# Quarter products of the last batch: one two-bank PSUM tile for two chains of sums, or a tile for each chain

## The chip, the cores and the metric

The kernel runs on one core of one Trainium2 chip. The metric is the device time in microseconds of one execution; the kernel before has a median of 998.69 us over three runs (998.07 to 1000.25). TensorE (PE) does the matrix products, its weight loads are shown as PEld; ScalarE (ACT) and VectorE (DVE) take results out of PSUM and do the arithmetic between products; GpSimd (POOL) and the DMA queues play no part in the stretch that is changed.

## The reference

Routing attention over 4 batches, 8 heads, 768 tokens of 64 numbers, followed by a two-layer network with a leaky slope per hidden unit:

```python
mask = q_assign[:, :, :, None] == k_assign[:, :, None, :]   # nearest of 16 centroids
scores = np.where(mask, scale * q @ k.T, -1e9)
attn = softmax(scores)
x = (attn @ v) as (3072, 512)
h = x @ w_in                                    # w_in  512 x 2048
g = np.maximum(h, 0.0) + alpha * np.minimum(h, 0.0)
out = g @ w_out                                 # w_out 2048 x 512
```

All of it is fp32.

## The kernel before, in words

The attention of one batch is computed while the two-layer network of the batch before it is fed in between in small pieces. The order of the instructions on each engine is the order of the program text (the pools are under a manual schedule); an engine executes its instructions in that order, and a tile pool adds the waits that its buffers and data need. Every buffer of a pool is given out in turn, and the first write to it waits until the last reader of its previous tile is done.

When the attention of all four batches has ended, the network of the last batch alone is left, and TensorE has nothing else to do. It is written by `last_pieces` (line 1089) and cuts each of the two matrix products in 2 x 2 quarters, so that seven quarter products are enough where eight would be needed, at the price of sums and differences on VectorE before and after. It has two stages.

**Hidden stage, `hidden(x)`, x = 0 to 7 ("blocks" here).** A block makes two tiles of 128 hidden units (x and 8 + x) for the 768 tokens of the batch, in halves of 384 tokens. It issues seven products. Each is two matmul instructions in the program and four matmul records in the trace (fp32), 128 x 384 wide. Two of the results are partial sums that are read out and then added to, in place, in PSUM:

- chain "a": products p1, p6, p7 and p4 into one PSUM area. p1 is copied out by ScalarE, then p6 is added to it and the sum is copied out by ScalarE, then p7 is added and VectorE adds the sum to a tile, then p4 is added and the last sum is copied out by ScalarE. Each read must be over before the next product of the chain writes.
- chain "e": products p5 and p3. p5 is copied out by ScalarE; p3 is added to it and VectorE adds the sum to a tile.
- "z": product p2 alone, which VectorE adds to a tile.

The order on TensorE is p1, p5, p2, p4 of the block before (it is put off by one block, list `late`), p6, p3, p7. Chains "a" and "e" are the two halves (bank 0 and bank 1) of one tile `two` of the pool `ps_s`, which has two such tiles; "z" comes from `ps_f`, which has two tiles of one bank.

VectorE does, for each block, in this order: the addition after p2, the slope (line 1129) of the block before after its p4, the addition after p3, a slope, the addition after p7, and then for x > 1 the sums that the second product needs of block x - 2: `g_sums` (4 operations, line 1168) and `w_out_sums` (4 operations, line 1177), and in blocks 2 and 4 also `w_in_sums` (4 wider ones, line 1080).

**Between the stages, `room_for_y`** runs the last p4 and the sums of blocks 6 and 7.

**Final stage, `final(t)`, t = 0 to 2.** Each t makes two row tiles of the output, again by seven products; here a product is 8 matmul instructions (16 records), 128 x 256 wide, one for each block x, in that order. The order is p1, p2, p5, p6, p3, p7 for t = 0 (p4 is put off into the next t), and p1, p5, p6, p2, p7, p3, p4 for t = 1 and 2. Chain "a" is p1, p6, p7, p4; chain "e" is p5, p3; "z" is p2. The copies are by ScalarE (line 1121), the additions by VectorE (line 1124), as before. p5 of t = 0 is the first product that reads what `g_sums` and `w_out_sums` made: its matmuls for x = 6 and x = 7 need the sums of `room_for_y`.

The pool `ps_v` (one tile of one bank) holds the attention's weighted sums and is not used in this part of the program before the change.

Of the kernel before, what the change touches and what calls it, by code (L numbers as in the profile page):

```python
# [10 lines left out]
FP32 = mybir.dt.float32  # L11
# [8 lines left out]
P = 128  # L20
# [3 lines left out]
def kernel(  # L24
# [20 lines left out]
    HS = HJ * P  # L45
# [26 lines left out]
    ps_s = fast.enter_context(tc.tile_pool(name="ps_s", bufs=2, space=PS))  # L72
    ps_v = fast.enter_context(tc.tile_pool(name="ps_v", bufs=1, space=PS))
    ps_m = fast.enter_context(tc.tile_pool(name="ps_m", bufs=1, space=PS))
    ps_f = fast.enter_context(tc.tile_pool(name="ps_f", bufs=2, space=PS))
# [984 lines left out]
    KH, NQ, HC = NCH // 2, NF // 2, DM // 2  # L1060
# [32 lines left out]
    def last_pieces():  # L1093
# [4 lines left out]
        def places():  # L1098
# [18 lines left out]
            s4.extend(t[:, h * HS:(h + 1) * HS] for t in more for h in range(2))  # L1117
            assert len(s4) >= NQ

        def copy(to, of):  # L1120
            nc.scalar.copy(to, of)

        def plus(to, of):
            nc.vector.tensor_tensor(out=to, in0=to, in1=of, op=ALU.add)
# [7 lines left out]
        def w_in_form(m, x, cc):  # L1132
            f1, f2 = (slice(f * P, (f + 1) * P) for f in (x, NQ + x))
            if m in ("11", "12"):
                return w_in_sb[:, cc + KH * (m == "12"), f1]
            if m in ("22", "S3"):
                return w_in_sb[:, cc + KH * (m == "22"), f2]
            t = by_pair[x // 2].rearrange("p (m c w) -> p m c w", m=3, c=KH)
            return t[:, ("S1", "S2", "S4").index(m), cc, (x % 2) * P:(x % 2 + 1) * P]

        def g_sum(x, m):

            if m == "S4":
                return s4[x]
            t = by_pair[x // 2].rearrange("p (x m q) -> p x m q", x=2, m=2)
            return t[:, x % 2, ("S1", "S2").index(m)]
# [8 lines left out]
        def w_out_form(m, x):  # L1155
            if m in ("11", "21", "22"):
                c0 = HC * (m == "22")
                return w_out_sb[:, x if m == "11" else NQ + x, c0:c0 + HC]
            i = ("T1", "T2", "T3", "T4").index(m)
            f = x + NQ * (i // 2)  # L1160
            return w_in_sb[:, KH * (i % 2):KH * (i % 2 + 1), f * P:(f + 1) * P]

        def g_sums(x):
            (t0, t1), (z0, z1) = g[x][0], g[NQ + x][0]
            S1, S2, S4 = (g_sum(x, m) for m in ("S1", "S2", "S4"))
            for to, p, q, op in ((S1, t1, z1, ALU.add), (S2, S1, t0, ALU.subtract),
                                 (t1, t0, t1, ALU.subtract), (S4, z0, S2, ALU.subtract)):
                nc.vector.tensor_tensor(out=to, in0=p, in1=q, op=op)

        def w_out_sums(x):  # L1170

            T1, T2, T3, T4 = (w_out_form(m, x) for m in ("T1", "T2", "T3", "T4"))
            B11, B12, B21, B22 = (
                w_out_sb[:, f, c0:c0 + HC].rearrange("p (a w) -> p a w", a=KH)
                for f in (x, NQ + x) for c0 in (0, HC))
            for to, p, q in ((T1, B12, B11), (T2, B22, T1), (T3, B22, B12), (T4, B21, T2)):
                nc.vector.tensor_tensor(out=to, in0=p, in1=q, op=ALU.subtract)
# [3 lines left out]
        def hidden(x):  # L1181
            f1, f2 = x, NQ + x
            bank = {}

            def product(to, m, rhs, start):
                if to == "a" and start:
                    two = ps_s.tile([P, 2, 512], FP32, name="sps")
                    bank["a"], bank["e"] = two[:, 0, 0:HS], two[:, 1, 0:HS]
                if to == "z":
                    bank["z"] = ps_f.tile([P, 512], FP32, name="fps")[:, 0:HS]  # L1190
                for cc in range(KH):
                    nc.tensor.matmul(out=bank[to], lhsT=w_in_form(m, x, cc),  # L1192
                                     rhs=rhs[:, cc, :], start=start and cc == 0,
                                     stop=cc == KH - 1, skip_group_check=not start)
                return bank[to]

            def x_of(half, kh):
                return xTs[b, half][:, kh * KH:(kh + 1) * KH]

            def g_of(f, half):  # L1200
                return g[f][0][half]

            def p1():
                if not g:
                    places()
                copy(g_of(f1, 0), product("a", "11", x_of(0, 0), True))

            def p5():
                copy(g_of(f2, 1), product("e", "S1", x_sums[0], True))

            def p2():
                plus(g_of(f1, 0), product("z", "12", x_of(0, 1), True))
                if late:
                    late.popleft()()

            def p6():
                copy(g_of(f1, 1), product("a", "S2", x_sums[1], False))

            def p3():
                plus(g_of(f1, 1), product("e", "S4", x_of(1, 1), False))  # L1220
                slopes(f1)

            def p7():
                plus(g_of(f2, 1), product("a", "S3", x_of(1, 0), False))
                late.append(p4)
                if x % 2 == 0 and x:
                    g_sums(x - 2)
                    w_out_sums(x - 2)
                    if x // 2 + 1 < NQ // 2:
                        w_in_sums(x // 2 + 1)  # L1230
                elif x > 1:
                    g_sums(x - 2)
                    w_out_sums(x - 2)

            def p4():
                copy(g_of(f2, 0), product("a", "22", x_sums[2], False))
                slopes(f2)
            return [p1, p5, p2, p6, p3, p7]

        def final(t):  # L1240
            bank = {}
            y0, y1 = (lambda c0, i=i: ys[i][:, c0:c0 + HC] for i in (t, HJ + t))

            def product(to, m, n, start):
                if to == "a" and start:
                    two = ps_s.tile([P, 2, 512], FP32, name="sps")
                    bank["a"], bank["e"] = two[:, 0, 0:HC], two[:, 1, 0:HC]
                if to == "z":
                    bank["z"] = ps_f.tile([P, 512], FP32, name="fps")[:, 0:HC]
                for x in range(NQ):  # L1250
                    nc.tensor.matmul(out=bank[to], lhsT=g_form(m, x, t),  # L1251
                                     rhs=w_out_form(n, x), start=start and x == 0,
                                     stop=x == NQ - 1, skip_group_check=not start)
                return bank[to]

            def store(i, c0, c1):
                nc.sync.dma_start(out=rows[:, i, c0:c1], in_=ys[i][:, c0:c1])

            def p1():
                copy(y0(0), product("a", "11", "11", True))  # L1260
                while late:
                    late.popleft()()

            def p5():
                copy(y1(HC), product("e", "S1", "T1", True))

            def p6():
                copy(y0(HC), product("a", "S2", "T2", False))

            def p2():  # L1270
                plus(y0(0), product("z", "12", "21", True))

            def p7():
                plus(y1(HC), product("a", "S3", "T3", False))
                if t == HJ - 1:
                    store(HJ + t, HC, DM)

            def p3():
                plus(y0(HC), product("e", "S4", "22", False))
                store(t, 0, DM)  # L1280

            def p4():
                copy(y1(0), product("a", "22", "T4", False))
                store(HJ + t, 0, HC if t == HJ - 1 else DM)
            if t == 0:
                return [p1, p2, p5, p6, p3, p7, lambda: late.append(p4)]
            return [p1, p5, p6, p2, p7, p3, p4]

        def room_for_y():
            late.popleft()()  # L1290
            t = xpool.tile([P, NCH, HS], FP32, name="xT").rearrange("p c q -> p (c q)")
            ys.extend(ypool.tile([P, DM], FP32, name="y") for _ in range(HJ))
            ys.extend(t[:, i * DM:(i + 1) * DM] for i in range(HJ))
            for x in (NQ - 2, NQ - 1):
                g_sums(x)
                w_out_sums(x)
        pieces = []
        for x in range(NQ):
            pieces += hidden(x)
        pieces.append(room_for_y)  # L1300
        for t in range(HJ):
            pieces += final(t)
# [246 lines left out]
    for i in (1, 3):  # L1549
# [25 lines left out]
                     start=True, stop=True)  # L1575
# [162 lines left out]
```

## Time and profile before

| what | before |
|---|---|
| median of 3 runs | 998.69 us |
| the profiled execution | 993.32 us, its span 991.5 us |
| PE busy | 952.9 us, 96% of the span |
| DVE busy / ACT busy | 69% / 26% |
| granted TensorE clock | 1.00 |
| hidden stage of the last batch | from 810.21 us to 904.92 us |
| final stage | from 904.92 us to 985.5 us |

The span is counted from the first to the last instruction of the profiled execution; that execution took 1.8 us more than its span, and its time is 5.4 us below the median of the timed runs. A row of the timeline gives the start, the length, the engine, the line, what is written and read, how many instructions are merged, and in square brackets how long the engine had been idle before it and who ended that. The lengths of matmuls are modelled and overlap: a product's own cost is read from the distance of two starts.

### The profile page before, as it was taken

The numbers are of one execution on the slowest core, as the hardware profiler recorded it, in microseconds if no ns is written. First come the engines' busy times: TensorE is split into PE (matmuls) and PEld (weight loads), VectorE is DVE, ScalarE is ACT, GpSimd is POOL, SyncE is SP. The second block draws the span as 40 slices with busy tenths as digits, with TensorE's granted clock in tenths as the row PEclk, the third lists the DMA queues.
The fourth block names the chain that finished last, engine by engine and source line by source line (L and its number), as shares of the span: only waits on it lengthen the run. The fifth ranks groups of instructions, "written<-read, shape, count | busy, mean of one in ns | idle before, by whom it ended". The sixth has DMA issues, their size and how long they took to land.

```text
span 991.5 us, 11208 instructions
## 1 busy us (share of the span) xinstructions
PE 952.9 (96%) x4059; PEld 498.9 (50%) x4059; DVE 684.0 (69%) x1241; ACT 259.5 (26%) x474; POOL 215.0 (22%) x249
## 2 busy tenths in 40 slices
PE   8999999999999999999999999999999998888997
PEld 5534444454454544545445454544545544446775
DVE  5897789798486886878867786687997353777000
ACT  5674534222220222302222022221322101111000
POOL 1432222110002624310000383510255410000000
PEclk9999999999999999999999999999999999999999
DMA  7442666080201654126020221803511120000000
GB/s 283 149 115 90 136 154 106 2 157 40 53 1 51 168 87 84 39 61 85 1 33 1 82 67 38 154 11 52 85 34 33 32 55 0 0 1 1 21 22 25
DMA packets 175583, 64.67 MB, mean 65 GB/s; under 512 B 161360, under 2 KB 165152, under 8 KB 175520
## 3 DMA queue, kind: packets, MB, share of 16 engines
q1 hardware_dynamic: 170064, 55.62, 25.4%
q0 software_dynamic: 4608, 7.87, 2.4%
q8 instruction: 34, 0.56, 0.2%
q10 hardware_dynamic: 848, 0.39, 0.2%
q14 instruction: 29, 0.24, 0.1%
HBM read 45.15 MB, written 18.35 MB: 64 GB/s over the span
## 4 chain that ended last, share of the span: by engine, by line
PE 89%; DVE 5%; ACT 2%; issue 1%; DMA 1%; POOL 0%; SPq 0%; DVEq 0%; ACTq 0%
PE fps L1017 25%; PE fps L1035 25%; PE vps L893 9%; PE sps L757 8%; PE sps L1192 7%; PE sps L1251 7%; PE fps L757 3%; PE fps L1251 1%; PE fps L1192 1%; DMA vt<-in_v_dram 1%; PE vps L926 1%; PE mps L381 1%; PE sps L766 1%; PE mps L926 1%; DVE power L265 0%
## 5 line engine op out<-in xcount | busy, mean ns | idle before, releaser
L1017 PE MATMUL fps<-xT,w_in_sb 128*128 128x384 f32 x768 | 259.2, 491 | 0.0
L1035 PE MATMUL fps<-w_out_sb,gT 128*128 128x512 f32 x576 | 256.0, 597 | 1.1 <-DVE gT L1009 1.1
L1017 PEld LDWEIGHTS fps<-xT,w_in_sb 128*128 128x128 f32 x768 | 142.3, 190 | 103.9 <-ACT more L778 4.4
L663 POOL DMA_INDIRECT scratch<-stage,off x96 | 102.3, 1066 | 323.2 <-DMA stage<-in_v_dram 269.5
L1035 PEld LDWEIGHTS fps<-w_out_sb,gT 128*128 128x128 f32 x576 | 106.9, 190 | 127.2 <-issue 117.4
L1023 ACT COPY gT<-fps 128x384 f32<-128x384 f32 x96 | 45.9, 478 | 224.2 <-PE fps L1017 224.2
L757 PE MATMUL sps<-qkT 64*128 64x384 f32 (+1 forms) x512 | 96.1, 494 | 0.0
L798 DVE SCALAR_TENSOR_TENSOR more<-aq,key,more 128x384 f32<-128x384 bf16 (+1 forms) x136 | 74.4, 605 | 29.5 <-ACT more L778 19.2
L1009 DVE SCALAR_TENSOR_TENSOR gT<-gT,alpha 128x384 f32<-128x384 f32 x96 | 61.3, 647 | 35.7 <-ACT gT L1023 35.5
L778 ACT ACTIVATE E<-sps 128x768 f32<-128x768 f32 (+1 forms) x81 | 61.2, 802 | 71.1 <-PE sps L766 38.4
L963 POOL DMA_INDIRECT back<-rows,place x48 | 47.5, 990 | 101.0 <-ACT rows L958 87.6
L757 PEld LDWEIGHTS sps<-qkT 64*128 64x128 f32 x512 | 45.7, 186 | 44.5 <-issue 17.4
L798 DVE SCALAR_TENSOR_TENSOR E<-aq,key,E 128x384 f32<-128x384 bf16 (+1 forms) x104 | 56.6, 601 | 16.1 <-ACT E L778 11.4
L893 PE MATMUL vps<-E,vt 128*64 128x384 f32 x356 | 65.7, 494 | 1.5 <-DVE xT L993 1.5
L808 DVE TENSOR_TENSOR acc<-acc,E 128x768 f32<-128x768 f32 x47 | 44.9, 955 | 14.8 <-ACT E L778 13.6
L778 ACT ACTIVATE more<-sps 128x768 f32<-128x768 f32 (+1 forms) x47 | 35.4, 796 | 41.3 <-PE sps L757 40.8
L271 POOL TENSOR_TENSOR w_in_sb<-w_in_sb,power 128x512 f32<-128x512 f32 x16 | 25.7, 1611 | 69.6 <-DVE w_in_sb L268 69.6
L893 PEld LDWEIGHTS vps<-E,vt 128*64 128x64 f32 x356 | 23.0, 136 | 33.4 <-issue 31.0
L893 PE MATMUL vps<-more,vt 128*64 128x384 f32 x220 | 38.8, 491 | 0.0
L1041 ACT COPY y<-fps 128x512 f32<-128x512 f32 x18 | 10.5, 586 | 101.2 <-PE fps L1035 101.2
L271 POOL TENSOR_TENSOR w_out_sb<-w_out_sb,power 128x512 f32<-128x512 f32 x16 | 22.5, 1410 | 56.0 <-DVE w_out_sb L268 56.0
L757 PE MATMUL fps<-qkT 64*128 64x384 f32 x160 | 34.5, 508 | 0.0
(267 smaller groups left out, 1072.9 us busy)
## 6 DMA issues: line engine op xcount, KB each, us to landing
raw<-in_moe_w_in_dram SPq DMA_DIRECT2D x16, 512.0 KB, 4.8
raw<-in_moe_w_out_dram SPq DMA_DIRECT2D x16, 512.0 KB, 3.8
out_dram<-y SPq DMA_DIRECT2D x21, 256.0 KB, 2.2
vt<-in_v_dram SPq DMA_DIRECT2D x12, 384.0 KB, 4.2
qk<-in_q_dram SPq DMA_DIRECT2D x48, 96.0 KB, 3.7
qk<-in_k_dram SPq DMA_DIRECT2D x48, 96.0 KB, 3.7
w_in_kept<-w_in_sb SPq DMA_DIRECT2D x8, 512.0 KB, 3.8
qk<-scratch SPq DMA_DIRECT2D x32, 96.0 KB, 3.4
```

The costliest lines, as they stand in the source:

```text
L271: nc.gpsimd.tensor_tensor(out=dst, in0=dst, in1=power[0].bitcast(FP32), op=ALU.mult)
L663: nc.gpsimd.indirect_dma_start(out=scratch[n][1][h * NX + xx], out_offset=bass.IndirectOffsetOnAxis(ap=ranks[n][:, xx, h:h + 1], axis=0), ...
L757: nc.tensor.matmul(out=bank(ps, h, m), lhsT=qkT[r:r + D, S + c * P:S + (c + 1) * P], rhs=qkT[r:r + D, tokens], start=True, stop=not early_ ...
L778: nc.scalar.activation(out=E[:, :, 0:m], in_=ps[:, :, 0:m], func=AF.Exp, scale=SCALE)
L798: nc.vector.scalar_tensor_tensor(out=e, in0=of, scalar=keys[n][:, NJ + c, h:h + 1], in1=e, op0=ALU.is_equal, op1=ALU.mult)
L893: nc.tensor.matmul(out=po[r:r + D, 0:HS], lhsT=vts[n][:, h, c, :], rhs=e[:, h, :], start=(c == 0), stop=(c == NJ - 1))
L963: nc.gpsimd.indirect_dma_start(out=to[i], out_offset=bass.IndirectOffsetOnAxis(ap=place[:, h, j:j + 1], axis=0), in_=rows[:, j, h * D:(h + ...
L1009: nc.vector.scalar_tensor_tensor(out=gs[f], in0=gs[f], scalar=alpha[:, f:f + 1], in1=gs[f], op0=ALU.mult, op1=ALU.max)
L1017: nc.tensor.matmul(out=ps[:, 0:HS], lhsT=w_in_sb[:, c, f * P:(f + 1) * P], rhs=xTs[b, half][:, c, :], start=(c == 0), stop=(c == NCH - 1))
L1035: nc.tensor.matmul(out=ps[:, 0:DM], lhsT=gs[f][:, i * P:(i + 1) * P], rhs=w_out_sb[:, f, :], start=on and f == f0, stop=off and f == f0 + ...
L1192: nc.tensor.matmul(out=bank[to], lhsT=w_in_form(m, x, cc), rhs=rhs[:, cc, :], start=start and cc == 0, stop=cc == KH - 1, skip_group_check ...
L1251: nc.tensor.matmul(out=bank[to], lhsT=g_form(m, x, t), rhs=w_out_form(n, x), start=start and x == 0, stop=x == NQ - 1, skip_group_check=no ...
```

## The change

The two chains no longer share a tile. Chain "a" takes one tile of `ps_s` and uses its first bank only; chain "e" takes the one tile of `ps_v`; "z" takes a tile of `ps_f` as before. This holds for both stages. In `room_for_y` the four `g_sums` operations of blocks 6 and 7 come first, and then the `w_out_sums` of both, where the two kinds alternated by block.

```diff
+        def new_bank(to):
+            if to == "a":
+                return ps_s.tile([P, 2, 512], FP32, name="sps")[:, 0, :]
+            pool, name = (ps_v, "vps") if to == "e" else (ps_f, "fps")
+            return pool.tile([P, 512], FP32, name=name)
...
             def product(to, m, rhs, start):
-                if to == "a" and start:
-                    two = ps_s.tile([P, 2, 512], FP32, name="sps")
-                    bank["a"], bank["e"] = two[:, 0, 0:HS], two[:, 1, 0:HS]
-                if to == "z":
-                    bank["z"] = ps_f.tile([P, 512], FP32, name="fps")[:, 0:HS]
+                if start:
+                    bank[to] = new_bank(to)[:, 0:HS]
...
             def product(to, m, n, start):
-                if to == "a" and start:
-                    two = ps_s.tile([P, 2, 512], FP32, name="sps")
-                    bank["a"], bank["e"] = two[:, 0, 0:HC], two[:, 1, 0:HC]
-                if to == "z":
-                    bank["z"] = ps_f.tile([P, 512], FP32, name="fps")[:, 0:HC]
+                if start:
+                    bank[to] = new_bank(to)[:, 0:HC]
...
             for x in (NQ - 2, NQ - 1):
                 g_sums(x)
+            for x in (NQ - 2, NQ - 1):
                 w_out_sums(x)
```

No product moves on TensorE, but what its products wait for does. Here is TensorE in block 3 of the hidden stage before the change, with the waits that stand in the program (an engine's name stands for a semaphore that it counts up); the rows are p1, p5, p2, p4 of block 2, p6, p3 and p7, and a product's second instruction is left out:

```order
L1192 MATMUL sps_5256<-xT_4756,w_in_sb_61 128x384 x2
L1192 MATMUL sps_5256<-vt_5096,qkT_5084 128x384 [waits Activation_49]
...
L1192 MATMUL fps_5263<-xT_4756,w_in_sb_61 128x384 x2
L1192 MATMUL sps_5218<-vt_5098,w_in_sb_61 128x384 [waits DVE_49]
...
L1192 MATMUL sps_5256<-vt_5097,qkT_5084 128x384 [waits Activation_49]
...
L1192 MATMUL sps_5256<-xT_4758,qkT_5084 128x384 [waits Activation_49]
...
L1192 MATMUL sps_5256<-xT_4758,w_in_sb_61 128x384 [waits DVE_49]
```

And the same products after it:

```order
L1195 MATMUL sps_5259<-xT_4756,w_in_sb_61 128x384 x2
L1195 MATMUL vps_5263<-vt_5096,qkT_5084 128x384 [waits DVE_49]
...
L1195 MATMUL fps_5267<-xT_4756,w_in_sb_61 128x384 x2
L1195 MATMUL sps_5220<-vt_5098,w_in_sb_61 128x384 [waits DVE_49]
...
L1195 MATMUL sps_5259<-vt_5097,qkT_5084 128x384 [waits Activation_49]
...
L1195 MATMUL vps_5263<-xT_4758,qkT_5084 128x384 [waits Activation_49]
...
L1195 MATMUL sps_5259<-xT_4758,w_in_sb_61 128x384 [waits Activation_49]
```

p5 no longer waits for ScalarE (the copy of p1, which reads the other half of the shared tile) but for VectorE: the one tile of `ps_v` must have been read by the addition after p3 of block 2. p7 no longer waits for VectorE (the addition after p3, other half) but for ScalarE: the copy of p6 in its own chain. p3 waits for ScalarE in both, before for the copy of p6, now for the copy of p5.

The second place is VectorE in `room_for_y`, before:

```order
L1168 TENSOR_TENSOR vt<-gT,qkT 128x384
L1177 TENSOR_TENSOR w_in_sb<-w_out_sb 128x2x128
L1177 TENSOR_TENSOR w_in_sb<-w_out_sb,w_in_sb 128x2x128
L1177 TENSOR_TENSOR w_in_sb<-w_out_sb 128x2x128
L1177 TENSOR_TENSOR w_in_sb<-w_out_sb,w_in_sb 128x2x128
L1168 TENSOR_TENSOR qkT<-gT 128x384
L1168 TENSOR_TENSOR qkT<-qkT,gT 128x384
L1168 TENSOR_TENSOR gT<-gT 128x384
L1168 TENSOR_TENSOR vt<-gT,qkT 128x384
L1177 TENSOR_TENSOR w_in_sb<-w_out_sb 128x2x128
```

and after:

```order
L1174 TENSOR_TENSOR vt<-gT,qkT 128x384
L1174 TENSOR_TENSOR qkT<-gT 128x384
L1174 TENSOR_TENSOR qkT<-qkT,gT 128x384
L1174 TENSOR_TENSOR gT<-gT 128x384
L1174 TENSOR_TENSOR vt<-gT,qkT 128x384
L1183 TENSOR_TENSOR w_in_sb<-w_out_sb 128x2x128
```

The first row is the end of `g_sums` of block 6. The first `w_out_sums` operation of block 6 stands four operations later than before, the first `g_sums` operation of block 7 four earlier, and the first `w_out_sums` operation of block 7 (the last row of the upper list) in the same place as before, as the ninth after the first row.

## The prediction

> **What bounds the kernel now.** I read the windows first, to see which engine limits the stretch that is changed, then PE's waits there, then the timeline for the price of each wait, and last VectorE's timeline, because the change hands it a wait. The first window is the network of the batch before, the second the hidden stage, the third the final stage.
>
> ```profile
> core 0: us, PE busy (x) PEld busy (x) DVE busy (x) ACT busy (x) POOL busy (x), PEclk, DMA share, GB/s
> 760.00:800.00 40.00, 39.47 (x145) 21.05 (x144) 20.23 (x35) 5.56 (x12) 21.42 (x22) 1.00 0.12 29
> 810.00:905.00 95.00, 79.53 (x228) 40.57 (x227) 54.54 (x110) 14.83 (x31) 0.00 (x0) 1.00 0.02 6
> 905.00:985.00 80.00, 74.77 (x336) 62.65 (x335) 13.46 (x33) 4.57 (x12) 0.00 (x0) 1.00 0.05 19
> ```
>
> PE is busy 39.47 of 40 us just before, then 79.53 of 95 and 74.77 of 80. No other engine is near full: VectorE has 54.54 of 95. So PE has gaps without a busier engine behind them; some chain goes to and fro between engines. PE's waits from 810 us on name it:
>
> ```profile
> engine line waited for: us in total, times, longest us
> PE sps L1192 <- ACT more L1121: 3.4, 6, 0.6
> PE sps L1192 <- ACT E L1121: 2.3, 4, 0.6
> ...
> PE sps L1192 <- DVE more L1124: 2.2, 3, 0.7
> PE sps L1251 <- DVE y L1124: 1.8, 3, 0.6
> ```
>
> PE waits for the engines that read its own results out of the shared tile, twice for ScalarE's copy and once for VectorE's addition in each hidden block. These idle times are too small as prices, since a matmul's modelled length overlaps the wait. The price is the distance of two starts less the product's own cost. Block 3, from p5 to the p5 of block 4:
>
> ```profile
> 846.31 1.56 PE L1192 MATMUL sps<-vt,qkT 128*128 128x384 f32 x4 [0.57 <-ACT more L1121]
> 847.71 1.45 PE L1192 MATMUL fps<-xT,w_in_sb 128*128 128x384 f32 x4
> 849.00 1.45 PE L1192 MATMUL sps<-vt,w_in_sb 128*128 128x384 f32 x4
> 850.28 1.45 PE L1192 MATMUL sps<-vt,qkT 128*128 128x384 f32 x4
> 852.31 1.56 PE L1192 MATMUL sps<-xT,qkT 128*128 128x384 f32 x4 [0.57 <-ACT more L1121]
> 854.58 2.85 PE L1192 MATMUL sps<-xT,w_in_sb 128*128 128x384 f32 x8 [0.72 <-DVE more L1124]
> 858.00 1.56 PE L1192 MATMUL sps<-vt,qkT 128*128 128x384 f32 x4 [0.57 <-ACT more L1121]
> ```
>
> A product costs 1.29 us (847.71 to 849.00 to 850.28). The block takes 858.00 - 846.31 = 11.69 us, seven products 9.03, so 2.66 us are lost. Split: p5 to p3 is four products, 5.16, and takes 6.00, so p3 loses 0.84; p3 to p7 takes 2.27 for 1.29, so p7 loses 0.98; p7 with the next p1 takes 3.42 for 2.58, so p5 loses 0.84.
>
> **The change, part by part.**
>
> *Hidden stage, three waits per block.* Each wait that is left after the change must be over before its product's turn. ScalarE first; the second copy is that of p6:
>
> ```profile
> 850.49 0.48 ACT L1121 COPY E<-sps 128x384 f32<-128x384 f32 x1 [2.10 <-PE sps L1192]
> 851.78 0.48 ACT L1121 COPY more<-sps 128x384 f32<-128x384 f32 x1 [0.81 <-PE sps L1192]
> ```
>
> p6 is through at 850.28 + 1.29 = 851.57, its copy ends at 852.26: 0.69 us later. After the change p7 waits for this copy with p3 between, 1.29 us: hidden with 0.6 to spare. ScalarE was idle 0.81 us before it, so it comes on time. p3 waits for the copy of p5 with p2, p4 and p6 between, 3.87 us; p6 for the copy of p1 with at least two products between. These vanish: p3 gains 0.84, p7 0.98.
>
> p5 now waits for VectorE's addition after the p3 of the block before, with p7 and p1 between, 2.58 us. In place of 0.84 us always, it pays only if VectorE is late. It is latest where its queue is longest, in blocks 3 and 5, after the sums that stand behind block 2 or 4. The timeline of that queue, first and last operations of each kind:
>
> ```profile
> 844.49 0.56 DVE L1124 TENSOR_TENSOR E<-E,sps 128x384 f32<-128x384 f32 x1 [0.59 <-PE sps L1192]
> 844.96 0.55 DVE L1168 TENSOR_TENSOR qkT<-more,more 128x384 f32<-128x384 f32 x1
> ...
> 846.96 0.42 DVE L1177 TENSOR_TENSOR w_in_sb<-w_out_sb 128x256 f32<-128x256 f32 x1
> ...
> 848.43 0.69 DVE L1080 TENSOR_TENSOR qkT<-w_in_sb 128x512 f32<-128x512 f32 x1
> ...
> 850.96 0.55 DVE L1124 TENSOR_TENSOR more<-more,fps 128x384 f32<-128x384 f32 x1
> 851.42 1.01 DVE L1129 SCALAR_TENSOR_TENSOR E<-E,alpha 128x768 f32<-128x768 f32 x1
> 853.97 0.55 DVE L1124 TENSOR_TENSOR more<-more,sps 128x384 f32<-128x384 f32 x1 [1.54 <-PE sps L1192]
> 854.56 1.02 DVE L1129 SCALAR_TENSOR_TENSOR more<-more,alpha 128x768 f32<-128x768 f32 x1
> 856.18 0.55 DVE L1124 TENSOR_TENSOR more<-more,sps 128x384 f32<-128x384 f32 x1 [0.60 <-PE sps L1192]
> ```
>
> From starts to starts: addition after p7 0.47, `g_sums` 2.00, `w_out_sums` 1.47, `w_in_sums` 2.53, addition after p2 0.46, slope 1.02, addition after p3 0.59, slope 1.02. Together 9.56 us, above PE's 9.03 in a block; but a block without `w_in_sums` has 7.03, so two blocks have 16.59 against 18.06, and VectorE catches up. Now count from the end of p7 of block 2 as zero, with PE unbroken. p3 ended at -1.29; the addition starts 0.37 later, as here (852.31 + 1.29 = 853.60 to 853.97), at -0.92; slope from -0.33 to 0.69; addition after p7 to 1.16; the twelve sums to 7.16; addition after p2 to 7.62; slope of block 2 to 8.64; then the addition after p3 of block 3 until 9.23. Its product was through at 6 x 1.29 = 7.74, so it is half a microsecond late. p5 of block 4 is due after eight products, at 10.32: 1.1 us to spare. I take nothing for this wait. Bounds: a gain is excluded, since PE cannot go below its products; the worst is that VectorE is late in all of the seven p5 behind a block, at the 0.98 us that a wait for this addition without cover costs now, 6.9 us.
>
> So eight blocks gain 8 x 2.66 = **21.3 us**.
>
> *Final stage.* Its first product, two that follow unbroken, one that waits, and its last product:
>
> ```profile
> 904.92 0.59 PE L1251 MATMUL sps<-w_out_sb,more 128*128 128x256 f32 x2
> ...
> 908.38 0.59 PE L1251 MATMUL fps<-w_out_sb,more 128*128 128x256 f32 x2
> ...
> 911.83 3.62 PE L1251 MATMUL sps<-w_in_sb,qkT 128*128 128x256 f32 x16
> 915.91 3.72 PE L1251 MATMUL sps<-w_in_sb,qkT 128*128 128x256 f32 x16 [0.46 <-ACT xT L1121]
> ...
> 981.79 0.70 PE L1251 MATMUL sps<-w_in_sb,more 128*128 128x256 f32 x2 [0.58 <-DVE y L1124]
> ```
>
> A product costs 3.45 us (904.92 to 908.38 to 911.83). The last of 21 starts 76.87 us after the first; twenty cost 69.1, so 7.8 us are lost, and 0.1 more inside the last, whose first two records take 0.70 where 0.59 is usual: 7.9 us. After the change every product of a chain has at least one product of another between itself and the one whose result must be read, 3.45 us, against 0.7 us (copy) or less than 1 us (addition). Gain **7.9 us**.
>
> *The turn between the stages.* p7 of block 7 is followed by its own p4, in chain "a", with nothing between. This wait stays:
>
> ```profile
> 900.72 0.56 DVE L1124 TENSOR_TENSOR gT<-gT,sps 128x384 f32<-128x384 f32 x1 [1.83 <-PE sps L1192]
> 901.19 1.14 DVE L1129 SCALAR_TENSOR_TENSOR gT<-gT,alpha 128x384 f32<-128x384 f32 x2
> 901.33 1.56 PE L1192 MATMUL sps<-xT,w_in_sb 128*128 128x384 f32 x4 [0.72 <-DVE gT L1124]
> 902.92 0.55 DVE L1124 TENSOR_TENSOR gT<-gT,sps 128x384 f32<-128x384 f32 x1 [0.59 <-PE sps L1192]
> 903.53 1.56 PE L1192 MATMUL sps<-vt,w_in_sb 128*128 128x384 f32 x4 [0.65 <-DVE gT L1124]
> ```
>
> p4 starts 2.20 after p7, 0.91 late. It grows: p7 will follow p3 at once, at 901.33 - 0.98 = 900.35, ending at 901.64, but VectorE has the slope in hand until 902.33. Its addition then starts at 902.33 instead of 901.64 + 0.30 = 901.94: **0.4 us lost**.
>
> *The reordered sums.* p5 of t = 0 started at 911.83 and ran unbroken to 915.28, so it waits for no sum now and nothing can be gained there. It needs the first `w_out_sums` operation of block 7 for its last two records, at 911.83 + 14 x 0.216 = 914.85; that operation is in its old place, and both VectorE's sums and PE's p4 start from the same addition, so the distance stays. The first operations of blocks 6 and 7 before:
>
> ```profile
> 909.92 0.42 DVE L1177 TENSOR_TENSOR w_in_sb<-w_out_sb 128x256 f32<-128x256 f32 x1
> ...
> 913.38 0.42 DVE L1177 TENSOR_TENSOR w_in_sb<-w_out_sb 128x256 f32<-128x256 f32 x1
> ```
>
> That of block 7 ends at 913.80, 1.0 us before its use. That of block 6 comes behind four more operations of 0.5 us, at 911.92 instead of 909.92, and is used at 911.83 + 12 x 0.216 = 914.42. I take zero; at worst p5 waits for the 1.5 us of one block's `w_out_sums`, and a gain is excluded.
>
> **Sum:** 21.3 + 7.9 - 0.4 = 28.8 us less. The profiled execution goes from 993.32 to 964.5 (span 991.5 to 962.7); its 5.4 us to the median I leave as it is: 998.69 - 28.8 = **969.9 us**.
>
> **The rivals.**
>
> *VectorE becomes the bound* through the one tile of chain "e". For it: 1.1 us to spare is little against a queue of 9.2. Against: over two blocks it has 1.5 us over, and no DMA or GpSimd work runs beside it. Price at most 6.9: 976.8.
>
> *One wait per block stays.* p7's cover has only 0.6 us to spare. If ScalarE's copy of p6 came after another, p7 would keep up to its 0.98: 8 x 0.98 = 7.8, 977.7. Against it stands the 0.81 us of idle time ahead of that copy.
>
> *The change does nothing:* the waits would be replaced by others just as long. 998.7. The instruction order speaks against it: the rows with waits have changed, and with them what is waited for.
>
> *Slower, by the clock.* The last stage has 56 x 1.29 + 21 x 3.45 = 144.7 us of products; closed up, they run without a rest. If the granted clock fell to c there, they would take 144.7 / c, and the gain would be gone below c = 144.7 / 173.5 = 0.83; at 0.80 the loss is 36.2, and 969.9 + 36.2 = 1006.1. Against it: 39.47 of 40 us busy at 1.00 in the window from 760 us. The Trainium skill (TensorE: Matmul & The Clock Gate, section "Seeing it yourself") knows a step to 13/16 once three cores of a die run dense matmuls; at that step 144.7 us would become 178.1 and the time 1003.3. It also says that one or two busy cores never trip it; by that this kernel, on one core, keeps its clock, and the trace agrees with 1.00.
>
> **How the numbers follow.** The forecast has 0.85, VectorE 0.06, the p7 wait 0.04, no change 0.02, the clock 0.03. The forecast's own range is 968 to 972.5, from the runs' spread of a microsecond and a half and the 1.5 us of the sums. Taking in half of VectorE's worst, 3.4 us, on top of it: **967.5 to 974**. About 0.2% (2 us) is what a measurement can tell from no change. Faster 0.95 (the first three cases), same 0.02, slower 0.03.
>
> **What would show it right or wrong.** Right: hidden blocks of about 9.0 us between two p5, final products 3.45 us apart, PE busy above 95% in both windows, no wait left at p3, p5 and p7, and one of about 1.3 us before the last p4 of the hidden stage. A wait of p5 for VectorE in blocks 4 and 6 would show the first rival; idle time before p7 for ScalarE the second; PEclk below 1.00 the last. The forecast is wrong if products get longer than 1.29 or 3.45 us while their waits are gone.

## The result and the profile after

The changed kernel takes 968.92 us (median of four executions, 968.76 to 969.34) against 998.6 us for the kernel before (four executions, 998.07 to 1000.25): a ratio of 0.9701, with a 95% interval of 0.9684 to 0.9718. That is 29.7 us less, with an interval of 28.2 to 31.6; forecast were 28.8 less. The profiled execution took 968.97 us, its span 967.2. PE is busy 946.1 us of it (98%), the granted clock is 1.00.

The windows of the hidden and the final stage in the kernel after, with the columns as in the prediction:

```profile
core 0: us, PE busy (x) PEld busy (x) DVE busy (x) ACT busy (x) POOL busy (x), PEclk, DMA share, GB/s
815.00:889.00 74.00, 73.05 (x228) 42.60 (x227) 53.59 (x110) 14.83 (x31) 0.00 (x0) 1.00 0.02 8
889.00:961.00 72.00, 72.00 (x335) 63.29 (x334) 13.71 (x33) 4.58 (x12) 0.00 (x0) 1.00 0.06 21
```

The same instructions (x228 on PE, x110 on VectorE) now fit into 74 us where they filled 95. PE is busy 73.05 of 74 us and 72.00 of 72. VectorE did the same work, 53.59 us where 54.54 stood, in less time, and it still has gaps. All of PE's waits from 810 us to the end, by line and releaser:

```profile
engine line waited for: us in total, times, longest us
PE sps L1195 <- DVE gT L1130: 0.9, 1, 0.9
```

One is left, where a long list stood. Block 3, from its p5 to the p5 of block 4, in PE's timeline (start, length, operation), and the p5 of block 5:

```profile
842.80 1.45 PE L1195 MATMUL vps<-vt,qkT 128*128 128x384 f32 x4
844.09 1.45 PE L1195 MATMUL fps<-xT,w_in_sb 128*128 128x384 f32 x4
845.38 1.45 PE L1195 MATMUL sps<-vt,w_in_sb 128*128 128x384 f32 x4
846.67 1.45 PE L1195 MATMUL sps<-vt,qkT 128*128 128x384 f32 x4
847.96 1.45 PE L1195 MATMUL vps<-xT,qkT 128*128 128x384 f32 x4
849.25 2.74 PE L1195 MATMUL sps<-xT,w_in_sb 128*128 128x384 f32 x8
851.83 1.45 PE L1195 MATMUL vps<-vt,qkT 128*128 128x384 f32 x4
...
860.86 1.45 PE L1195 MATMUL vps<-vt,qkT 128*128 128x384 f32 x4
```

From p5 to p5 it is 851.83 - 842.80 = 9.03 us, and 9.03 again to 860.86: seven products of 1.29 and nothing else, where the block took 11.69. In the final stage the first three products and the last one:

```profile
889.17 0.59 PE L1251 MATMUL sps<-w_out_sb,more 128*128 128x256 f32 x2
...
892.62 0.59 PE L1251 MATMUL fps<-w_out_sb,more 128*128 128x256 f32 x2
...
896.08 3.62 PE L1251 MATMUL vps<-w_in_sb,qkT 128*128 128x256 f32 x16
...
958.24 0.59 PE L1251 MATMUL sps<-w_in_sb,more 128*128 128x256 f32 x2
```

The last of the 21 products starts 958.24 - 889.17 = 69.07 us after the first: twenty times 3.45, where it was 76.87.

To compare executions whatever happened earlier in them, the experiments use two distances of starts in the trace. The *hidden distance* goes from the first matmul of the hidden stage to the first of the final stage; the *final distance* goes from there to the last matmul record. In the kernel before they are 94.72 and 80.21 us, after the change 73.77 and 72.30: together 28.85 us less.

### The profile page after: what moved, and what is told of

It reads as the page before. It is cut to its first block, busy times and chain, and to the rows that moved or that the text cites. A ratio compares the mean times of both kernels' runs of the same rounds, so it can differ in the third digit from the quotient of the medians.

```text
span 967.2 us, 11202 instructions
## 1 busy us (share of the span) xinstructions
PE 946.1 (98%) x4059; PEld 502.8 (52%) x4059; DVE 683.5 (71%) x1241; ACT 260.0 (27%) x474; POOL 213.2 (22%) x249
## 4 chain that ended last, share of the span: by engine, by line
PE 92%; DVE 5%; issue 1%; ACT 1%; POOL 0%; DVEq 0%; ACTq 0%; POOLq 0%
PE fps L1035 25%; PE fps L1017 25%; PE vps L893 9%; PE sps L757 8%; PE sps L1251 4%; PE sps L1195 4%; PE fps L757 3%; PE vps L1251 2%; PE vps L1195 2%; PE fps L1251 1%; PE fps L1195 1%; PE mps L381 1%; PE mps L926 1%; PE vps L926 1%; PE sps L766 1%
```

## Experiments

| run | median us | ratio to before (95%) | hidden distance | final distance |
|---|---|---|---|---|
| after | 968.92 | 0.9701 (0.9684 to 0.9718) | 73.77 | 72.30 |
| before, profiled again | 998.69 | 1.0013 (0.9989 to 1.0036) | 94.72 | 80.20 |
| hidden stage alone | 976.49 | 0.9785 (0.9767 to 0.9803) | 73.77 | 80.20 |
| final stage alone | 990.02 | 0.9919 (0.9903 to 0.9936) | 94.72 | 72.30 |
| old order of sums | 968.74 | 0.9700 (0.9684 to 0.9716) | 73.77 | 72.30 |
| 1 more wide sum | 967.41, one execution | | 73.77 | 72.30 |
| 2 more wide sums | 969.96, one execution | | 74.17 | 72.30 |
| 4 more wide sums | 970.95, one execution | | 77.08 | 72.30 |
| last p4 later | 968.04 | 0.9692 (0.9663 to 0.9722) | 71.27 | 73.59, p4 in it |

### The kernel before, profiled again

The kernel before is unchanged. The question is the 5.4 us between its profiled execution (993.32) and its median (998.69), which the forecast left as it was.

> The kernel before, unchanged, for a second profile of it. Its timed runs were 998.07 to 1000.25 us but its one profiled execution took 993.32 us, and in the changed kernel's profile the first matmul of the last batch starts 5.2 us later (815.39 against 810.21 us), nearly all of it in one place near 725 us where PE, ACT and DVE idle at once with no releaser shown. Theory (that place differs from execution to execution and has nothing to do with the change): this profile shows the place too, the first matmul of the last batch starts near 815.4 us and the time is near 998.5 us; the last two stages last 94.7 and 80.6 us as before. Rival (the change moved something ahead of its stage): the start stays at 810.2 us.

The profiled execution took 998.29 us, as the median does. Its two stages have the distances of the first profile to 0.01 us, but the hidden stage starts at 815.12 us and not at 810.21. The 4.9 us are lost ahead of the stretch that is changed. A window around the place where the two executions part, for the first profile of the kernel before:

```profile
720.00:734.00 14.00, 13.05 (x77) 7.34 (x74) 12.76 (x25) 5.58 (x11) 4.38 (x5) 1.00 0.21 40
```

for its second profile:

```profile
720.00:734.00 14.00, 12.47 (x68) 6.66 (x67) 9.49 (x21) 4.93 (x9) 5.27 (x6) 1.00 0.21 42
```

and for the kernel after:

```profile
720.00:734.00 14.00, 11.51 (x66) 6.55 (x65) 8.09 (x18) 4.82 (x9) 4.52 (x5) 1.00 0.22 42
```

In the first profile VectorE is busy 12.76 of the 14 us, in the second 9.49, in that of the kernel after 8.09. So the first profile shows an execution without an idle place that the other one of the same kernel has, and every other trace here. The longest wait of ScalarE there, in the second profile, names no engine of the core as releaser:

```profile
ACT more L778 <- remote: 3.7, 1, 3.7
```

What stands behind that is open. It has nothing to do with the change: two executions of one kernel differ in it. To set the stages apart from it, compare the second profile with that of the kernel after: 998.29 - 968.97 = 29.32 us, of which the stages are 28.85; the hidden stage starts 0.27 later after the change, and the stretch from the last matmul record to the end of the span is 0.68 shorter (5.71 against 6.39), and the 0.06 left lie around the span. That stretch lies between 5.56 and 6.39 us in all the runs, with no order that goes with the edits.

### The hidden stage alone

The change without its part in `final` and without the new order of the sums:

```diff
 # in final(t), as it was before the change
-                if start:
-                    bank[to] = new_bank(to)[:, 0:HC]
+                if to == "a" and start:
+                    two = ps_s.tile([P, 2, 512], FP32, name="sps")
+                    bank["a"], bank["e"] = two[:, 0, 0:HC], two[:, 1, 0:HC]
+                if to == "z":
+                    bank["z"] = ps_f.tile([P, 512], FP32, name="fps")[:, 0:HC]
 # in room_for_y
-            for x in (NQ - 2, NQ - 1):
                 w_out_sums(x)
```

> Own tiles for the two chains in the hidden stage only; the final stage and the order of the last sums as before. Theory (the terms add up): the hidden stage falls from 94.7 to 73.8 us, the final stage stays with its 7.9 us of waits; time 998.6 - 20.9 = 977.7 us. Rival (what is gained in the first stage is lost again in the second, because VectorE arrives there late): above 980 us.

The ratio 0.9785 of 998.49 us is 21.5 us less (by its interval 19.7 to 23.3; 20.9 were expected). The hidden distance is that of the change, the final distance that of the kernel before. Of PE's waits the ones of line 1254, the final stage, are back, and only the p4 of the turn is left of line 1195:

```profile
PE sps L1254 <- DVE y L1130: 1.7, 3, 0.6
PE sps L1254 <- ACT xT L1127: 1.4, 3, 0.5
PE sps L1254 <- DVE xT L1130: 1.2, 2, 0.6
PE sps L1195 <- DVE gT L1130: 0.9, 1, 0.9
PE sps L1254 <- ACT y L1127: 0.9, 2, 0.5
```

### The final stage alone

The reverse: `hidden(x)` as before the change, with the old order of the sums, and `final(t)` with tiles of its own for each chain.

```diff
 # in hidden(x), as it was before the change
-                if start:
-                    bank[to] = new_bank(to)[:, 0:HS]
+                if to == "a" and start:
+                    two = ps_s.tile([P, 2, 512], FP32, name="sps")
+                    bank["a"], bank["e"] = two[:, 0, 0:HS], two[:, 1, 0:HS]
+                if to == "z":
+                    bank["z"] = ps_f.tile([P, 512], FP32, name="fps")[:, 0:HS]
 # in room_for_y
-            for x in (NQ - 2, NQ - 1):
                 w_out_sums(x)
```

> Own tiles for the two chains in the final stage only; the hidden stage and the order of the last sums as before. Theory: the hidden stage stays at 94.7 us, the final stage loses its 7.9 us of waits; time 998.6 - 7.9 = 990.7 us. Rival as for the run with the hidden stage alone: the two do not add up to 28.8 us.

It is 8.1 us faster than before (0.9919; by its interval 6.4 to 9.7 us, 7.9 were expected). Its waits are those of the hidden stage, line 1198 here, and none of the final one:

```profile
PE sps L1198 <- ACT more L1127: 3.4, 6, 0.6
...
PE sps L1198 <- DVE more L1130: 2.1, 3, 0.7
...
PE sps L1198 <- ACT gT L1127: 1.1, 2, 0.6
```

The two halves are independent: their distances add up to those of the whole change without a rest, (94.72 - 73.77) + (80.20 - 72.30) = 20.95 + 7.90 = 28.85 us. Each half was undone by going back to the shared tile and nothing else but the order of the sums, which the next run shows to be worth nothing; so the shared tile is what made the waits.

### The old order of the sums

The whole change, but `g_sums` and `w_out_sums` alternate by block as they did before.

```diff
             for x in (NQ - 2, NQ - 1):
                 g_sums(x)
-            for x in (NQ - 2, NQ - 1):
                 w_out_sums(x)
```

> The changed kernel with the order of the last sums put back (by block: the four inner sums, then the four of the second weights). Theory (p5 of the first t waits for the sum that stands in the same place in both orders, and has 1 us to spare): same time as the changed kernel, 968.9 us, no idle time before that p5. Rival (the reorder is part of the gain, since VectorE is closer behind PE now): up to 1.5 us more, with a wait of p5 or p6 for VectorE.

Both distances are those of the change to 0.01 us, and p5 of t = 0 runs in one piece of 3.62 us, its row as short as that of the change:

```profile
896.24 3.62 PE L1251 MATMUL vps<-w_in_sb,qkT 128*128 128x256 f32 x16
```

The new order of the sums is worth nothing here, in either direction. The whole gain is that of the tiles.

### One, two or four more sums on VectorE

These three ask how far VectorE is from becoming the bound. In blocks 2 and 4 the first of the wide sums is done again one, two or four times, with the same operands and result; the output does not change. The extra operations stand in VectorE's queue ahead of the addition that p5 of the block after the next waits for.

```diff
 # in w_in_sums; again = 1, 2 or 4
-        for to, x, y, op in ((S1, A21, A22, ALU.add), (S2, S1, A11, ALU.subtract),
+        again = 4 if p > 1 else 0
+        for to, x, y, op in ((S1, A21, A22, ALU.add),) * (1 + again) + (
+                             (S2, S1, A11, ALU.subtract),
```

One more:

> The changed kernel with VectorE's queue made longer where it is longest: the first of the four wide sums for the weight pairs 2 and 3 (behind p7 of blocks 2 and 4) is done twice, 0.6 to 0.7 us more each time. It leaves the result as it is. Theory (p5 of blocks 4 and 6 has 1.1 us to spare): no wait before any p5, the hidden stage stays at 73.8 us. Rival (the wait for VectorE is already at its limit): p5 of blocks 4 and 6 each lose up to 0.7 us, stage up to 75.2 us.

Two more:

> The same with that sum done three times, 1.2 to 1.4 us more in each of the two places. Theory (1.1 us to spare): p5 of blocks 4 and 6 wait for VectorE, 0.1 to 0.3 us each; stage 74.0 to 74.4 us. Rival (the order of VectorE does not matter, since a result is taken out in time anyway): no wait.

Four more:

> The same with that sum done five times, 2.4 to 2.8 us more in each of the two places. Theory (1.1 us to spare): p5 of blocks 4 and 6 wait for VectorE, 1.3 to 1.7 us each, and no other product does; stage 76.4 to 77.2 us. Rival (no limit by VectorE): stage 73.8 us.

Five such operations in VectorE's timeline, with four more sums, and the one behind them, give the price of one:

```profile
844.78 3.59 DVE L1082 TENSOR_TENSOR qkT<-w_in_sb 128x512 f32<-128x512 f32 x5
848.40 0.69 DVE L1082 TENSOR_TENSOR qkT<-qkT,w_in_sb 128x512 f32<-128x512 f32 x1
```

(848.40 - 844.78) / 5 = 0.72 us each, 2.90 for four. On PE, in the same kernel, p7 of block 3 with p1 of block 4 in one row, and then p5 of block 4:

```profile
848.08 2.74 PE L1197 MATMUL sps<-xT,w_in_sb 128*128 128x384 f32 x8
852.21 1.56 PE L1197 MATMUL vps<-vt,qkT 128*128 128x384 f32 x4 [1.39 <-DVE more L1132]
```

The p5 was due at 848.08 + 2.58 = 850.66 and starts at 852.21, 1.55 late. 2.90 less 1.55 is 1.35 us that VectorE had to spare. The same place in PE's timeline with two more sums:

```profile
849.60 2.74 PE L1197 MATMUL sps<-xT,w_in_sb 128*128 128x384 f32 x8
852.27 1.56 PE L1197 MATMUL vps<-vt,qkT 128*128 128x384 f32 x4
```

Due at 852.18, started at 852.27, 0.09 late: 1.45 - 0.09 = 1.36. With one more, 0.72, the distances are those of the change and no p5 waits. The slope behind the addition that p5 needs, and that p5, with one more sum:

```profile
849.00 1.02 DVE L1137 SCALAR_TENSOR_TENSOR more<-more,alpha 128x768 f32<-128x768 f32 x1
...
849.64 1.45 PE L1197 MATMUL vps<-vt,qkT 128*128 128x384 f32 x4
```

The addition is through when the slope starts, 0.64 us before p5: 0.72 + 0.64 = 1.36. The three agree on 1.35 us to a few hundredths. The hidden distance says the same in sum: with four more it grows by 3.31 us, two places of 1.55 and 0.10 each (the 0.10 is the longer first record, below); with two more by 0.40, two of 0.09 and 0.10. The times of these three, one execution each, do not tell them apart; the distances do. p5 does come to wait for VectorE as the first rival had it, but only from 1.35 us of work more in each of the two places. The expected waits (0.1 to 0.3 us with two more, 1.3 to 1.7 with four) and stages came out close to what was measured partly by luck: an added sum costs 0.72 us and not 0.6 to 0.7, the slack is 1.35 and not 1.1, and the two errors cancel. With 0.72 and 1.1 the count would have given 0.35 and 1.8.

### The last p4 later

The one wait that is left is that of p4 of block 7. Here p4 is put off by one more product, behind p1 of the first t of the final stage, and the sums that need its result go there with it, alternating between blocks 6 and 7:

```diff
 # w_out_sums, which can now do a part of its four operations
-        def w_out_sums(x):
+        def w_out_sums(x, part=slice(0, 4)):
...
 # in room_for_y
-            late.popleft()()
...
-            for x in (NQ - 2, NQ - 1):
-                g_sums(x)
-            for x in (NQ - 2, NQ - 1):
-                w_out_sums(x)
+            g_sums(NQ - 2)
 # in final(t), after p1 and the products that were put off
+                if t == 0:
+                    g_sums(NQ - 1)
+                    for i in range(4):
+                        for x in (NQ - 2, NQ - 1):
+                            w_out_sums(x, slice(i, i + 1))
```

> The changed kernel with the last p4 of the hidden stage put behind p1 of the final stage, so that the addition after p7 has 3.4 us of another product to hide behind; VectorE's sums of block 6 go ahead of the slope that waits for p4, and the last sums of the second weights are done in the order of their use. Theory (the one wait that the change left is of the same kind and costs 1.2 us in the changed kernel): no wait before p4, none before p5, 1.2 us less: 967.7 us, which the times can hardly tell from 968.9; the distance from the first matmul of the hidden stage to the last of the final one tells it. Rival (the wait only moves, since p5 of the first t must now wait for later sums): the distance stays within 0.3 us, and p2 or p5 show a wait for VectorE.

PE has no wait left from 808 us to the end. p7, p1, p4, p2 and p5 in its timeline:

```profile
886.80 1.45 PE L1195 MATMUL sps<-xT,w_in_sb 128*128 128x384 f32 x4
888.09 0.59 PE L1251 MATMUL sps<-w_out_sb,more 128*128 128x256 f32 x2
...
891.54 1.45 PE L1195 MATMUL sps<-vt,w_in_sb 128*128 128x384 f32 x4
892.83 0.59 PE L1251 MATMUL fps<-w_out_sb,more 128*128 128x256 f32 x2
...
896.28 3.62 PE L1251 MATMUL vps<-w_in_sb,qkT 128*128 128x256 f32 x16
```

p1 follows p7 after 1.29 us, p4 follows p1 after 3.45, p2 follows p4 after 1.29, and p5 is not broken by the sums. Both distances together are 144.86 us, 1.22 less than after the change: the wait of 1.11 us and 0.10 of the longer record. That is close to its products alone, 56 x 1.29 + 21 x 3.45 less the last record's 0.22, or about 144.5; of the rest 0.32 are two small matmuls that the program has between blocks 0 and 1, of another part, and the longer record behind them:

```profile
823.27 1.45 PE L1195 MATMUL sps<-xT,w_in_sb 128*128 128x384 f32 x4
824.65 0.19 PE L1576 MATMUL mps<-ones,good 128*1 128x1 f32 x2
824.77 1.56 PE L1195 MATMUL sps<-xT,w_in_sb 128*128 128x384 f32 x4
826.17 1.45 PE L1195 MATMUL vps<-vt,qkT 128*128 128x384 f32 x4
```

From p7 to the p5 of block 1 it is 826.17 - 823.27 = 2.90 us where two products cost 2.58. The time, 0.9692 (0.9663 to 0.9722), cannot be told from 0.9701; that it is faster by those 1.2 us is shown by the trace alone.

## Why the prediction was right, point by point

**Hidden stage, 21.3 us: right in cause and size.** The block is 9.03 us long, as forecast. p3, p7 and p5 no longer wait. p7's new wait for the copy of p6 is covered as said: the copy starts at 848.16, and p7 goes at 849.25 without a wait. ScalarE's rows around it in the kernel after:

```profile
843.00 0.48 ACT L1127 COPY more<-sps 128x384 f32<-128x384 f32 x1 [3.39 <-PE sps L1195]
...
848.16 0.48 ACT L1127 COPY more<-sps 128x384 f32<-128x384 f32 x1 [0.81 <-PE sps L1195]
```

It is through at 848.64, 0.61 us before p7 starts; "hidden with 0.6 to spare" is what the row says. The copy at 843.00 is that of p1, and now lies under p5, which starts at 842.80 and is followed by the next product 1.29 us later: reading one bank while PE writes another costs PE nothing here. The Trainium skill (PSUM — Partial Sum Buffer, section "Summary: rules for kernel authors") says to read a different bank from the one a matmul writes, and to guard by bank; this trace agrees with it. Before the change p1 and p5 lay in different banks too, but of one tile, and the wait that the program held was for the tile.

The eight blocks gave 21.2 rather than 21.3: of the 2.66 us of a block 0.10 is the longer first record of its p7, which the count charged to the p5 behind it, and the first block has no p7 ahead of its p5.

**p5's new wait: right that it costs nothing, its slack under-sized.** Said were 1.1 us to spare. VectorE in the kernel after, first at p7 of block 2, where the count begins, then around the addition after p3 of block 3:

```profile
840.22 2.74 PE L1195 MATMUL sps<-xT,w_in_sb 128*128 128x384 f32 x8
840.49 0.56 DVE L1130 TENSOR_TENSOR E<-E,vps 128x384 f32<-128x384 f32 x1 [1.12 <-PE vps L1195]
...
848.94 1.01 DVE L1135 SCALAR_TENSOR_TENSOR E<-E,alpha 128x768 f32<-128x768 f32 x1
849.87 0.55 DVE L1130 TENSOR_TENSOR more<-more,vps 128x384 f32<-128x384 f32 x1
850.45 1.02 DVE L1135 SCALAR_TENSOR_TENSOR more<-more,alpha 128x768 f32<-128x768 f32 x1
```

The addition is through when the slope behind it starts, at 850.45, and p5 starts at 851.83: 1.38 us, and 1.35 by the added sums. The count took 1.02 for a slope, the length of its row, "from starts to starts"; the distance of starts is 849.87 - 848.94 = 0.93, since VectorE begins the next operation before the row of the last has ended. The count holds two slopes, 0.09 too long each. It also took the addition after p3 of block 2 to start 0.37 us after its product, as before the change; here that product is through at 840.22, where p7 starts, and the addition starts at 840.49, 0.27 later. The 0.10 is the longer first record that p3 had behind its wait and now, without one, has not. Two slopes and this are 0.28 of the 0.29 us between 1.09 and 1.38.

**Final stage, 7.9 us: right.** The distance shrank by 80.21 - 72.30 = 7.91, and with the final stage alone by as much.

**The turn, 0.4 us lost: right in cause, the size was 0.2.** The turn in the kernel after, PE and VectorE:

```profile
885.37 1.45 PE L1195 MATMUL sps<-xT,w_in_sb 128*128 128x384 f32 x4
...
886.11 1.14 DVE L1135 SCALAR_TENSOR_TENSOR gT<-gT,alpha 128x384 f32<-128x384 f32 x2
887.17 0.55 DVE L1130 TENSOR_TENSOR gT<-gT,sps 128x384 f32<-128x384 f32 x1
...
887.77 1.56 PE L1195 MATMUL sps<-vt,w_in_sb 128*128 128x384 f32 x4 [0.95 <-DVE gT L1130]
```

p4 starts 2.40 us after p7, 1.11 late, where 0.91 stood before and about 1.3 were forecast. The chain is the one that the prediction gave: the slope is in VectorE's hand when p7's sum is ready. Two terms were mis-sized. The slope was taken by its row, 1.14, where its follower starts after 887.17 - 886.11 = 1.06. And p7 was moved up by 0.98 while VectorE's slope was left at its old time; but 0.10 of that 0.98 is p3's own longer first record, without which p3's sum, and so the slope, comes 0.10 earlier as well. Together they are 0.18 of the 0.20 us between 1.31 and 1.11. With the 21.2 us of the blocks, 21.2 - 0.2 = 21.0 is the 20.95 that the hidden distance shrank by. That the whole, 28.8 us forecast and 28.85 measured, comes closer than its terms is luck: the gain of the blocks was put 0.1 too high and the loss at the turn 0.2 too high, and they pull opposite ways.

**Reordered sums, zero: right,** shown by the run with the old order.

**The rivals.** VectorE as the bound fell, and its distance was measured. The p7 wait did not stay. "The change does nothing" fell. The clock in both stages is 1.00, with PE busy 73.05 of 74 and 72.00 of 72 us, so "slower, by the clock" fell too. The Trainium skill (TensorE: Matmul & The Clock Gate, section "Seeing it yourself") ties the step to 13/16 to three busy cores of a die; on this one core it does not show in either stage.

**The 5.4 us "left as it is": right to leave, by luck.** No reason was given for it. They are an idle place 85 us ahead of the stage, which the profile of before happened not to have. Had they been in the stages, the sum against that profile would have been off by as much. What is left between the forecast and the median, 0.9 us of 29.7, is inside the interval of the ratio and is not resolved.

## What to carry to other kernels

When two chains of sums are read out and added to in turn, give each its own tile: here a tile over two banks made each chain wait for the reader of the other, and with tiles of their own one product of another chain between write and read (1.29 us) covered the whole way out by ScalarE (0.69 us). Price such a wait by the distance of starts less the product (0.84 and 0.98 us), not by the idle time in the row (0.57 and 0.72), and price an engine's queue by distances of starts too, not by row lengths. Before trusting that a queue with little to spare holds, lengthen it by a known operation until it doesn't: that gave the 1.35 us to a few hundredths.

## What was not expected of the hardware

**A product that starts after a wait is 0.10 us longer.** p4 behind its wait has a row of 1.56 us and the next product starts 887.77 + 1.40; p4 put off behind p1, without a wait, has 1.45 and 1.29 (891.54 to 892.83). The same holds for p5 with four more sums (1.56, and it starts late by 1.55 while the stage grows by 1.65). So each of the waits removed here gave 0.10 us more than its lateness. A wait is not the only thing that brings it: behind the two small matmuls between blocks 0 and 1, where the profile names no wait, the row is 1.56 as well.

**An idle place near 725 us** in which PE, ScalarE and VectorE have gaps together, stands in all traces but the first of the kernel before (there the hidden stage begins at 810.21 us, in the second 4.9 us later, in all the others at 813.2 us or later), and in some of them the granted clock falls there, as in the same window of the run with the old order of the sums:

```profile
720.00:734.00 14.00, 11.78 (x63) 6.98 (x63) 8.77 (x21) 5.03 (x9) 4.21 (x5) 0.88 0.21 40
```

It is 0.88 in four of the traces and 1.00 in the others, with no relation to the edits that can be seen. No run here shows the cause of the place or of the lower clock in it; both stay open.
